# Reordering the start, the statistics, one weight load and the output products of a fused attention and gated-MLP kernel

**Chip, cores, metric.** One core of a Trainium2 chip. The metric is the device time of one execution in microseconds (us); lower is better. A profile's span is about 1.8 us shorter than the time of the same execution.

## The reference

Layernorm of x (2048 x 640, bf16), then the sum of three branches: x itself; a linear attention with 32 heads of 20; a gated MLP (640 to 1536 and back).

```python
xn = layernorm(x)                                  # over 640, no weights
q, k, v = split(xn @ wqkv)                         # 32 heads of 20
phi(t) = concat(softmax(t @ w_phi), softmax(-(t @ w_phi)))
o = (phi(q) @ (phi(k).T @ v)) / (phi(q) @ sum(phi(k)) + 1e-6)
out = x + o @ wo + (silu(xn @ w1) * (xn @ w3)) @ w2
```

## The kernel before, cut to the parts that matter

Tokens are worked in tiles of 128 (`t`, 16 of them) and chunks of 512 (`c`, four). Chunk 0 is normalized and transposed on chip by TensorE; chunks 1 to 3 are normalized, stored to DRAM and read back by a transposing DMA. A list scheduler in the kernel fixes each engine's order at build time; TensorE takes its units in program order. Six PSUM banks go around. One gate unit `GU(c, fi)` is ten products of 128x512: `gs` on VectorE frees the gate's bank.

```python
    def setup():
        ...
        for t in range(0, 4, 2):                       # x tiles 0..3, two queues
            load_x(xg[0], t // 2, 1, 0)                 # SP
            load_x(xg[0], 2 + t // 2, 1, 0, nc.scalar)  # ACT
        nc.sync.dma_start(out=wv[:], in_=wqkv3[:, :, 2 * D : 3 * D])   # V's weights, 800 KB
        load_gu(0)                                      # gate and up weights, part 0
        nc.sync.dma_start(out=wrow[:], ...)
        nc.sync.dma_start_transpose(out=wkT[:], in_=A_wqkv[:, D : 2 * D])
    def later():
        load_x(xg[1], 0, 4, 1)                          # second x chunk, 640 KB
        load_gu(2); load_gu(3)
    WARM = 11                                           # dummy products
    # ... [cut: layernorm of tile 0..3, T(t) = transposes of tile t, interleaved]
    T(0, "ACT"); T(1, "ACT")
    V(0); T(2, "DVE"); V(1); T(3, "DVE")
    plan.op("ACT", 0.5, lambda: load_gu(1, nc.scalar))  # part 1, issued from ScalarE's queue
    plan.op("SP", 0.5, later)
    V(2); V(3)
    # ... transposing load of wqT, then w2 (1.92 MB), both on SP
    fill(3 * 2.16)                                      # gate units 0..2
    for t in range(4, 8):
        ln_stats(t, ("g", 0, t // 2 - 2))               # second chunk, behind gs 0, 0, 1, 1
    for u in prep("k", wkT, wkphi, 13.0):               # folding products, ten units
        u(); fill(0.4)
    for t in range(NST):
        K(t)
        if t == 0 or t == 5 or t == 9:
            LN((t + 3) // 4 if t else 1, t)             # normalize, store, transposed read
        # ... gate units, V(t), KV(t - 2)
    KV(NST - 2)
    for g in range(4): Q(0, g)
    KV(NST - 1)
    def O(t):                                           # output tile
        for half, (lo, hi) in enumerate(zip(edges, edges[1:])):
            # 12 products with w2, then 5 with wo, into one bank, then the addition and the store
            ...
```

The softmax here doesn't subtract the row's maximum and nothing guards it: scores larger than these inputs give would overflow.

## Time and profile before

| | kernel before |
|---|---|
| median of the first 4 runs | 281.26 us (281.06 to 282.76) |
| profiled span | 279.5 us |
| TensorE busy | 270.8 us, 97% |
| TensorE idle | 8.7 us |
| first gate product | 14.69 us |

The lines themselves, and how they are read, are in the prediction. One warning for later: this is one execution, and the first 14 us of this kernel turned out to differ from execution to execution (the first gate product came at 13.79 to 17.97 us in five traces with this start).

### The profile page before, as it was taken

Reading aid. Unit: us, or ns where it says so; the run is one execution under the profiler, and the core shown is the slowest. Engines: PE = TensorE matmul, PEld = TensorE weight load, DVE = VectorE, ACT = ScalarE, POOL = GpSimd, SP = SyncE. Lnnn points to the kernel's source line nnn. Section 1 sums busy time; section 2 is a strip of 40 time slices with the busy share of each in tenths; the row PEclk is TensorE's granted clock in tenths of the full one; section 3 lists DMA queues with packets and bytes.
Section 4 is the critical chain, followed back from the end, with each engine's and each line's share of the span. In section 5 each row is a group of like instructions: output and inputs, shape, how many; then the busy total and the mean of one; then the engine's idle time right before and its main releaser. Section 6 shows DMA issues by size and latency. Waiting matters only on the chain.

```text
span 279.5 us, 4928 instructions
## 1 busy us (share of the span) xinstructions
PE 270.8 (97%) x1904; PEld 165.2 (59%) x1904; DVE 172.8 (62%) x285; ACT 147.0 (53%) x320; POOL 94.8 (34%) x124
## 2 busy tenths in 40 slices
PE   7897999999999999999999999999999999999995
PEld 2644555555566655557555577567665676467774
DVE  5507599999667974665639965732937229426421
ACT  3755776666677666667688723833228332532000
POOL 8264557775557453655212200001010110330000
PEclk9999999999999999999999999999999999999999
DMA  7999995202700060000300362261030621300311
GB/s 222 249 333 255 255 340 126 85 2 94 188 2 0 2 185 3 2 0 8 113 0 2 95 104 94 67 163 69 30 91 23 137 85 41 95 0 26 114 50 49
DMA packets 44103, 26.56 MB, mean 95 GB/s; under 512 B 26416, under 2 KB 44080, under 8 KB 44080
## 3 DMA queue, kind: packets, MB, share of 16 engines
q1 hardware_dynamic: 42336, 24.90, 33.3%
q10 hardware_dynamic: 1744, 1.34, 1.6%
q8 instruction: 15, 0.25, 0.4%
q14 instruction: 8, 0.07, 0.1%
HBM read 12.81 MB, written 7.21 MB: 72 GB/s over the span
## 4 chain that ended last, share of the span: by engine, by line
PE 80%; DVE 6%; DMA 5%; SPq 4%; ACT 2%; issue 1%; DVEq 0%; ACTq 0%
PE bank L557 31%; PE bank L801 18%; PE bank L406 12%; PE bank L805 8%; PE bank L645 6%; DMA xg<-in_A_x_dram 3%; SPq L176 3%; PE bank L691 1%; PE rtbank L691 1%; DMA oT<-od 1%; DVE gs L578 1%; DVE phik L471 1%; PE kva L490 1%; PE bank L514 1%; PE kvb L490 1%
## 5 line engine op out<-in xcount | busy, mean ns | idle before, releaser
L557 PE MATMUL bank<-xnT,w 128*128 128x512 bf16 x480 | 109.8, 379 | 0.2 <-DVE gs L578 0.2
L601 POOL TENSOR_TENSOR hT<-gs,up 128x512 bf16<-128x512 bf16 x44 | 51.2, 1164 | 139.7 <-ACT up L596 84.1
L557 PEld LDWEIGHTS <-w 128*128 128x128 bf16 x480 | 46.6, 98 | 50.4 <-issue 0.4
L801 PE MATMUL bank<-w,hT 128*128 128x320 bf16 (+2 forms) x396 | 57.9, 295 | 0.0
L573 ACT ACTIVATE th<-bank 128x512 bf16<-128x512 f32 x48 | 29.1, 607 | 36.7 <-PE bank L557 36.6
L578 DVE SCALAR_TENSOR_TENSOR gs<-th,bank 128x512 bf16<-128x512 bf16 x48 | 32.5, 676 | 24.2 <-ACT th L573 24.1
L801 PEld LDWEIGHTS <-hT 128*128 128x128 bf16 x396 | 38.0, 98 | 14.6
L406 PEld LDWEIGHTS <-xnT 128*128 128x128 bf16 x320 | 30.5, 98 | 14.0 <-issue 1.1
L810 DVE TENSOR_TENSOR res<-bank,xr 128x320 bf16<-128x320 f32 (+2 forms) x33 | 15.8, 479 | 36.3 <-PE bank L805 36.3
L596 ACT ACTIVATE up<-bank 128x512 bf16<-128x512 f32 x44 | 26.6, 603 | 22.2 <-PE bank L557 21.6
L454 DVE TENSOR_REDUCE ks<-ek 128x64 f32<-128x1280 bf16 x16 | 23.6, 1476 | 16.9 <-ACT ek L445 16.9
L471 POOL TENSOR_TENSOR phik<-ek,kr 128x640 bf16<-128x640 bf16 x16 | 29.1, 1820 | 8.4 <-PE bank L406 3.0
L699 ACT CAST rt<-bank 128x352 bf16<-128x352 f32 x32 | 13.1, 468 | 30.2 <-PE bank L691 26.4
L805 PE MATMUL bank<-wo,oT 128*128 128x320 bf16 (+2 forms) x165 | 27.1, 295 | 0.3 <-DMA oT<-od 0.3
L406 PE MATMUL bank<-wv,xnT 128*128 128x320 bf16 x160 | 24.2, 299 | 1.0 <-DMA wv<-in_A_wqkv_dram 1.0
L445 ACT ACTIVATE ek<-bank 128x320 bf16<-128x320 f32 x64 | 23.1, 437 | 3.7 <-PE bank L406 3.5
L406 PE MATMUL bank<-wkphi,xnT 128*128 128x320 bf16 x160 | 24.3, 299 | 0.0
L471 DVE TENSOR_TENSOR phik<-ek,kr 128x640 bf16<-128x640 bf16 x16 | 22.1, 1383 | 1.8 <-PE bank L406 0.5
L660 ACT ACTIVATE eq<-bank 128x512 bf16<-128x512 f32 x40 | 21.8, 601 | 2.8 <-PE bank L645 2.6
L645 PE MATMUL bank<-xnT,wqphi 128*128 128x512 bf16 x100 | 22.7, 379 | 0.0
L805 PEld LDWEIGHTS <-oT 128*128 128x128 bf16 x165 | 15.8, 98 | 6.4 <-DMA oT<-od 0.6
L287 DVE BATCH_NORM_STATS2 stats<-xg 128x6 f32<-128x320 bf16 x32 | 14.0, 471 | 6.1 <-DMA xg<-in_A_x_dram 6.1
(63 smaller groups left out, 212.6 us busy)
## 6 DMA issues: line engine op xcount, KB each, us to landing
w<-in_B_w_dram SPq DMA_DIRECT2D x6, 480.0 KB, 9.6
xr<-in_A_x_dram SPq DMA_DIRECT2D x4, 640.0 KB, 4.6
od<-om SPq DMA_DIRECT2D x8, 320.0 KB, 2.3
out_dram<-res SPq DMA_DIRECT2D x15, 160.0 KB, 1.8
w<-in_B_w_dram SPq DMA_DIRECT2D x1, 1920.0 KB, 10.8
xnd<-xn SPq DMA_DIRECT2D x3, 640.0 KB, 3.2
xg<-in_A_x_dram SPq DMA_DIRECT2D x10, 160.0 KB, 3.3
w<-in_B_w_dram ACTq DMA_DIRECT2D x2, 480.0 KB, 4.9
```

The costliest lines, as they stand in the source:

```text
L406: nc.tensor.matmul(o["ps"][:], xnT[:, c, t * P : (t + 1) * P], w[:, c, 320 * half : 320 * half + 320], start=(c == 0), stop=(c == KD - 1),)
L445: nc.scalar.activation(out=box["ek"][:, sgn, 320 * half : 320 * half + 320], in_=o["ps"][:], func=AF.Exp, scale=1.0 - 2.0 * sgn,)
L454: nc.vector.reduce_sum(out=box["s"][:].rearrange("p a h -> p (a h)"), in_=box["ek"][:].rearrange("p a (h d) -> p (a h) d", d=Dh), axis=AX.X,)
L471: phik_ins[t] = eng.tensor_mul(out=phik_b[t][:, :, sgn, :], in0=box["ek"][:, sgn, :].rearrange("p (h d) -> p h d", d=Dh), in1=box["r"][:, ...
L557: nc.tensor.matmul(o["ps"][:], w[:, k, fi * P : (fi + 1) * P], xs[:, k, :], start=(k == 0), stop=(k == KD - 1))
L573: nc.scalar.activation(out=box["th"][:], in_=og["ps"][:], func=AF.Tanh, scale=0.5)
L578: pinned["g", c, fi] = nc.vector.scalar_tensor_tensor(out=box["gs"][:], in0=box["th"][:], scalar=1.0, in1=og["ps"][:], op0=ALU.add, op1=AL ...
L596: nc.scalar.activation(out=box["up"][:], in_=ou["ps"][:], func=AF.Copy, scale=0.5)
L601: lambda: nc.gpsimd.tensor_mul(out=hT[c][:, fi, :], in0=box["gs"][:], in1=box["up"][:]),
L645: nc.tensor.matmul(o["ps"][:], wqphi[:, k, g * P : (g + 1) * P], xnT[:, k, c * 512 : (c + 1) * 512], start=(k == 0), stop=(k == KD - 1),)
L801: nc.tensor.matmul(o["ps"][:], hT[c][:, fi, ti * P : (ti + 1) * P], w2[:, fi, cols], start=(fi == 0), stop=False)
L805: nc.tensor.matmul(o["ps"][:], oT[c][:, k, ti * P : (ti + 1) * P], wo_of[0][:, k, cols], start=False, stop=(k == KD - 1))
```

## The change

Its intent is to start TensorE's useful work sooner, to take the waits out of the first 30 us, and to put ready products ahead of two later waits.

```diff
 setup():
-        for t in range(0, 4, 2):
-            load_x(xg[0], t // 2, 1, 0); load_x(xg[0], 2 + t // 2, 1, 0, nc.scalar)
-        nc.sync.dma_start(out=wv[:], ...)
+        # tile 0 in two halves, one on each queue
+        load_x(xg[0], 1, 1, 0)
+        load_x(xg[0], 2, 1, 0, nc.scalar)
+        load_wv(0)
+        load_wv(1)
+        load_x(xg[0], 3, 1, 0)
         load_gu(0)
         # wrow
+        load_gu(1)                       # now on SP, ahead of wkT
         # transposing load of wkT
         load_x(xg[1], 0, 4, 1); load_gu(2); load_gu(3)
@@ dummies: 11 -> 10, then 4 behind T(0) and 2 behind T(1); T(0) copied out in two parts
-    V(0); T(2, "DVE"); V(1); T(3, "DVE")
+    # V(0) first half, T(1), V(0) second half, V(1) first half, T(2, "ACT"), V(1) second half, T(3)
-    plan.op("ACT", 0.5, lambda: load_gu(1, nc.scalar))
@@ statistics of the second chunk
-    for t in range(4, 8): ln_stats(t, ("g", 0, t // 2 - 2))
     for u in prep("k", ...): u(); fill(0.4)
     # LN(1), the normalization of this chunk, moves from K(0) to behind the last of the gates below
+    fill((6 - gi) * 2.16)
+    for t in range(4, 8): ln_stats(t, ("g", 0, t - 2))
@@ w2
-    plan.op("SP", 0.5, <load w2>, after=36.0)
+    # behind LN(1): issued only after the transposed read of chunk 1
+            plan.op("SP", 0.5, load_w2, deps=[XT_of[4]])
@@
+    Q(0, 0)
     KV(NST - 2)
-    for g in range(4): Q(0, g)
+    for g in range(1, 4): Q(0, g)
@@ O(t), all tiles but the last
-        half 0: 12 x w2, 5 x wo;  half 1: 12 x w2, 5 x wo
+        half 0: 12 x w2;  half 1: 12 x w2;  half 0: 5 x wo;  half 1: 5 x wo
```

More of the change, by code (lines that the diff above doesn't have):

```diff
@@ L159, in load_x, with load_gu, load_wv @@
         )
-    def load_gu(i, queue=nc.sync):
+    def load_gu(i):
         for w, src in zip((w1, w3), w13):
-            queue.dma_start(out=w[:, :, 384 * i : 384 * i + 384], in_=src[:, :, 384 * i : 384 * i + 384])
+            nc.sync.dma_start(out=w[:, :, 384 * i : 384 * i + 384], in_=src[:, :, 384 * i : 384 * i + 384])
+    def load_wv(h):
+        nc.sync.dma_start(
+            out=wv[:, :, 320 * h : 320 * h + 320],
+            in_=wqkv3[:, :, 2 * D + 320 * h : 2 * D + 320 * h + 320],
+        )
     def setup():
@@ L168, in setup @@
         xg[1] = five.tile([P, 4, D], bf, name="xg", tag="five")
-        nc.vector.memset(xg[0][:, 2, 0:8], 0.0)
-        for t in range(0, 4, 2):
-            load_x(xg[0], t // 2, 1, 0)
-            load_x(xg[0], 2 + t // 2, 1, 0, nc.scalar)
-        nc.sync.dma_start(out=wv[:], in_=wqkv3[:, :, 2 * D : 3 * D])
+        nc.vector.memset(xg[0][:, 0, 320:328], 0.0)
+        nc.sync.dma_start(out=xg[0][:, 0, 0:320], in_=x2[0:P, 0:320])
+        nc.scalar.dma_start(out=xg[0][:, 0, 320:640], in_=x2[0:P, 320:640])
+        load_x(xg[0], 1, 1, 0)
[3 more added lines that the diff above has]
+        load_x(xg[0], 3, 1, 0)
         load_gu(0)
         nc.sync.dma_start(out=wrow[:], in_=A_w_phi.rearrange("h j f -> (h j) f").rearrange("(g p) f -> p g f", p=P))
+        load_gu(1)
         nc.sync.dma_start_transpose(out=wkT[:], in_=A_wqkv[:, D : 2 * D])
-    def later():
         load_x(xg[1], 0, 4, 1)
@@ L206, in warm, with dummies @@
     def warm():
-        nc.vector.memset(xnT[:, 0, 0:512], 0.0)
-        ps = bank([P, 512], f32)
-        for i in range(WARM):
-            nc.tensor.matmul(ps[:], xnT[:, 0, 0:P], xnT[:, 0, 0:512])
-    WARM = 11
+        nc.vector.memset(xnT[:, KD - 1, S - 512 : S], 0.0)
+        warm_ps.append(bank([P, 512], f32))
+        dummies(10)
+    warm_ps = []
+    def dummies(n):
+        for i in range(n):
+            nc.tensor.matmul(warm_ps[0][:], xnT[:, KD - 1, S - P : S], xnT[:, KD - 1, S - 512 : S])
     def constants():
@@ L270 @@
     rstd = consts.tile([P, NST], f32, name="rstd")
-    arrive = [3.0, 3.4, 3.8, 4.2] + [15.0] * 4
+    arrive = [3.0, 3.4, 3.8, 4.2] + [19.0] * 4
     stats_of = {}
@@ L354, in LN, with tr @@
         )
-        xt = plan.op(
-            "SP", 0.5,
-            lambda: nc.sync.dma_start_transpose(out=xnT[:, :, 512 * c : 512 * c + 512], in_=xn_d[c][:]),
-            deps=[st], lat=5.0,
-        )
+        def tr():
+            pinned["xnT", c] = nc.sync.dma_start_transpose(
+                out=xnT[:, :, 512 * c : 512 * c + 512], in_=xn_d[c][:]
+            )
+        xt = plan.op("SP", 0.5, tr, deps=[st], lat=5.0)
         for t in range(4 * c, 4 * c + 4):
@@ L375, in bank, with T, fn, ev @@
         return ringp.tile(shape, dt, name="bank", tag="bank")
-    def T(t, evac):
+    def T(t, evac, parts=((0, KD),)):
         dep = apply_of[t]
-        o = {}
-        def fn():
-            o["ps"] = bank([P, D], bf)
-            for c in range(KD):
-                nc.tensor.transpose(o["ps"][:, c * P : (c + 1) * P], xn[0][:, t, c * P : (c + 1) * P], ident[:])
-        u = plan.op("PE", pe_us(KD, P), fn, deps=[dep], takes="bank", frees=[xn_of[0]])
-        def ev():
-            dst = xnT[:, :, t * P : (t + 1) * P]
-            src = o["ps"][:].rearrange("p (c s) -> p c s", c=KD)
-            if evac == "DVE":
-                nc.vector.tensor_copy(out=dst, in_=src)
-            else:
-                nc.scalar.copy(out=dst, in_=src)
-        XT_of[t] = plan.op(evac, dve_us(D, 2) if evac == "DVE" else act_us(D), ev, deps=[u], frees=[u])
+        for lo, hi in parts:
+            o = {}
+            def fn(o=o, lo=lo, hi=hi):
+                o["ps"] = bank([P, (hi - lo) * P], bf)
+                for c in range(lo, hi):
+                    nc.tensor.transpose(
+                        o["ps"][:, (c - lo) * P : (c - lo + 1) * P], xn[0][:, t, c * P : (c + 1) * P], ident[:]
+                    )
+            u = plan.op("PE", pe_us(hi - lo, P), fn, deps=[dep], takes="bank", frees=[xn_of[0]])
+            def ev(o=o, lo=lo, hi=hi):
+                dst = xnT[:, lo:hi, t * P : (t + 1) * P]
+                src = o["ps"][:].rearrange("p (c s) -> p c s", c=hi - lo)
+                if evac == "DVE":
+                    nc.vector.tensor_copy(out=dst, in_=src)
+                else:
+                    nc.scalar.copy(out=dst, in_=src)
+            n = (hi - lo) * P
+            XT_of[t] = plan.op(evac, dve_us(n, 2) if evac == "DVE" else act_us(n), ev, deps=[u], frees=[u])
     V_of, phik_of, KV_of, phik_b, phik_a = {}, {}, {}, {}, {}
@@ L411, in proj, with V_half, V_evac, ev @@
         return plan.op("PE", pe_us(KD, 320), fn, deps=deps, takes="bank", frees=frees), o
-    def V(t, halves=(0, 1)):
-        V_of.setdefault(t, [])
-        for half in halves:
-            u, o = proj(t, wv, half, [XT_of[t]], [big_of["wv"]])
-            def ev(o=o, half=half):
-                nc.scalar.copy(
-                    out=vaug[t % 4][:, 16 * half : 16 * half + 16, 0:Dh],
-                    in_=o["ps"][:].rearrange("p (h d) -> p h d", d=Dh),
-                )
-            V_of[t].append(plan.op("ACT", act_us(320), ev, deps=[u, KV_of.get(t - 4)], frees=[u]))
+    def V_half(t, half):
+        return proj(t, wv, half, [XT_of[t]], [big_of["wv"]])
+    def V_evac(t, half, units):
+        u, o = units[t, half]
+        def ev():
+            nc.scalar.copy(
+                out=vaug[t % 4][:, 16 * half : 16 * half + 16, 0:Dh],
+                in_=o["ps"][:].rearrange("p (h d) -> p h d", d=Dh),
+            )
+        V_of.setdefault(t, []).append(
+            plan.op("ACT", act_us(320), ev, deps=[u, KV_of.get(t - 4)], frees=[u])
+        )
+    def V(t):
+        for half in range(2):
+            V_evac(t, half, {(t, half): V_half(t, half)})
     wphi_ready = {}
@@ L793, in O, with products, fn, ev @@
         edges = (0, 320, 512, 640) if last else (0, 320, 640)
-        for half, (lo, hi) in enumerate(zip(edges, edges[1:])):
-            cols = slice(lo, hi)
-            o = {}
-            def fn(o=o, cols=cols, lo=lo, hi=hi):
-                o["ps"] = bank([P, hi - lo], f32)
-                for fi in range(KF):
-                    nc.tensor.matmul(
-                        o["ps"][:], hT[c][:, fi, ti * P : (ti + 1) * P], w2[:, fi, cols], start=(fi == 0), stop=False
-                    )
-                for k in range(KD):
-                    nc.tensor.matmul(o["ps"][:], oT[c][:, k, ti * P : (ti + 1) * P], wo_of[0][:, k, cols], start=False, stop=(k == KD - 1))
-            u = plan.op("PE", pe_us(KF + KD, hi - lo), fn, deps=GU_of[c] + [dep, wo_dma], takes="bank", frees=[oT_a[c], hT_a[c]])
-            def ev(o=o, cols=cols, half=half):
-                nc.vector.tensor_tensor(out=box["res"][:, cols], in0=o["ps"][:], in1=xr[c][:, ti, cols], op=ALU.add)
+        outs = []
+        def products(half, wo):
+            lo, hi = edges[half : half + 2]
+            o = outs[half]
+            def fn():
+                if not wo:
+                    o["ps"] = bank([P, hi - lo], f32)
+                    for fi in range(KF):
+                        nc.tensor.matmul(
+                            o["ps"][:], hT[c][:, fi, ti * P : (ti + 1) * P], w2[:, fi, lo:hi],
+                            start=(fi == 0), stop=False,
+                        )
+                else:
+                    for k in range(KD):
+                        nc.tensor.matmul(
+                            o["ps"][:], oT[c][:, k, ti * P : (ti + 1) * P], wo_of[0][:, k, lo:hi],
+                            start=False, stop=(k == KD - 1),
+                        )
+            if not wo:
+                o["u"] = plan.op("PE", pe_us(KF, hi - lo), fn, deps=GU_of[c], takes="bank", frees=[hT_a[c]])
+                return
+            u = plan.op("PE", pe_us(KD, hi - lo), fn, deps=[dep, wo_dma, o["u"]], frees=[oT_a[c]])
+            def ev():
+                nc.vector.tensor_tensor(
+                    out=box["res"][:, lo:hi], in0=o["ps"][:], in1=xr[c][:, ti, lo:hi], op=ALU.add
+                )
                 if half == 1:
@@ L814, in ev @@
                 elif half == 2:
-                    nc.scalar.dma_start(out=out2[t * P : (t + 1) * P, cols], in_=box["res"][:, cols])
-            plan.op("DVE", dve_us(hi - lo), ev, deps=[u, xr_of[c], rb], frees=[u, xr_a[c]] + [rb] * (half == len(edges) - 2))
+                    nc.scalar.dma_start(out=out2[t * P : (t + 1) * P, lo:hi], in_=box["res"][:, lo:hi])
+            plan.op(
+                "DVE", dve_us(hi - lo), ev, deps=[u, xr_of[c], rb],
+                frees=[o["u"], xr_a[c]] + [rb] * (half == len(edges) - 2),
+            )
+        for half in range(len(edges) - 1):
+            outs.append({})
+            products(half, False)
+            if last:
+                products(half, True)
+        for half in range(0 if last else 2):
+            products(half, True)
     xr_of = {}
@@ L827, in residual, with load_w2 @@
         xr_of[c] = plan.op("SP", 0.5, lambda: load_x(xr[c], 0, 4, c), deps=[xr_a[c]], lat=3.5)
+    def load_w2():
+        order_after(
+            nc.sync.dma_start(out=w2[:], in_=B_w2.rearrange("(c p) d -> p c d", p=P)), pinned["xnT", 1]
+        )
     wo_of = []
@@ L841 @@
     ln_sqrt(1)
-    T(0, "ACT")
+    T(0, "ACT", ((0, 2), (2, KD)))
+    plan.op("PE", 0.8, lambda: dummies(4))
     ln_stats(2, parts=(0,))
@@ L846 @@
     ln_sqrt(2)
+    v = {(0, 0): V_half(0, 0)}
     T(1, "ACT")
+    plan.op("PE", 0.4, lambda: dummies(2))
+    v[0, 1] = V_half(0, 1)
+    V_evac(0, 0, v)
     ln_stats(3, parts=(0,))
@@ L851 @@
     ln_sqrt(3)
-    plan.op("ACT", 1.3, lambda: nc.scalar.preload_act_table(AF.Exp), deps=[rstd_of[3]])
-    V(0)
-    T(2, "DVE")
-    V(1)
+    V_evac(0, 1, v)
+    v[1, 0] = V_half(1, 0)
+    T(2, "ACT")
+    v[1, 1] = V_half(1, 1)
     ln_finish(3)
     T(3, "DVE")
-    plan.op("ACT", 0.5, lambda: load_gu(1, nc.scalar))
-    plan.op("SP", 0.5, later)
+    plan.op("ACT", 1.3, lambda: nc.scalar.preload_act_table(AF.Exp), deps=[rstd_of[3]])
+    V_evac(1, 0, v)
+    V_evac(1, 1, v)
     V(2)
@@ L864 @@
     plan.op("SP", 0.5, lambda: nc.sync.dma_start_transpose(out=wqT[:], in_=A_wqkv[:, 0:D]), after=24.0)
-    plan.op("SP", 0.5, lambda: nc.sync.dma_start(out=w2[:], in_=B_w2.rearrange("(c p) d -> p c d", p=P)), after=36.0)
     def modes(n):
@@ L885 @@
     fill(3 * 2.16)
-    for t in range(4, 8):
-        ln_stats(t, ("g", 0, t // 2 - 2))
     for u in prep("k", wkT, wkphi, 13.0):
@@ L890 @@
         fill(0.4)
+    fill((6 - gi) * 2.16)
+    for t in range(4, 8):
+        ln_stats(t, ("g", 0, t - 2))
     wq_seq = prep("q", wqT, wqphi, 34.0)
@@ L895 @@
             fetch(7 + t, t)
-        if t == 0 or t == 5 or t == 9:
-            LN((t + 3) // 4 if t else 1, t)
+        if t == 5 or t == 9:
+            LN((t + 3) // 4, t)
         fill(1.95)
+        if t == 0:
+            LN(1, ("g", 0, gi - 1))
+            plan.op("SP", 0.5, load_w2, deps=[XT_of[4]])
         if t >= 4:
@@ L908 @@
     fill(2.2)
+    Q(0, 0)
     KV(NST - 2)
-    for g in range(4):
+    for g in range(1, 4):
         Q(0, g)
```

## The prediction

> **What bounds the kernel now.** I read the engine totals first, then every wait of TensorE, then the order of work in the first 30 us, then the DMA landings there.
>
> ```profile
> PE 270.8 (97%) x1904; PEld 165.2 (59%) x1904; DVE 172.8 (62%) x285; ACT 147.0 (53%) x320; POOL 94.8 (34%) x124
> PE   7897999999999999999999999999999999999995
> DMA  7999995202700060000300362261030621300311
> ```
>
> TensorE is busy 270.8 of 279.5 us and is the only engine near full, so only two things can shorten the span: idle time of TensorE, and work that it does for nothing. The idle time is 279.5 - 270.8 = 8.7 us. The list of TensorE's waits names most of it:
>
> ```profile
> PE bank L514 <- DVE gs L578: 1.9, 1, 1.9
> PE bank L210 <- DVE xnT L207: 1.3, 1, 1.3
> PE bank L406 <- DMA wv<-in_A_wqkv_dram: 1.0, 1, 1.0
> PE bank L384 <- DVE xn L332: 0.6, 1, 0.6
> PE kva L490 <- DVE phik L471: 0.4, 1, 0.4
> PE bank L805 <- DMA oT<-od: 0.3, 1, 0.3
> PE bank L557 <- DVE gs L578: 0.2, 1, 0.2
> ```
>
> These add up to 5.7 us. The rest is the tail: TensorE's last product ends at 275.99 + 0.44 = 276.43 us, so 3.1 us of addition and store follow. 5.7 + 3.1 is the 8.7 within rounding. The work for nothing is the 11 warm-up products (4.9 us), run while the first x tile is on its way. The start, as TensorE's timeline has it:
>
> ```profile
> 1.27 4.88 PE L210 MATMUL bank<-xnT 128*128 128x512 bf16 x11 [1.27 <-DVE xnT L207]
> 5.94 0.74 PE L384 MATMUL bank<-ident,xn 128*128 128x128 bf16 x5
> 8.71 1.52 PE L406 MATMUL bank<-wv,xnT 128*128 128x320 bf16 x10 [0.98 <-DMA wv<-in_A_wqkv_dram]
> ```
>
> The first gate product starts at 14.69 us; from there TensorE is full but for the small waits. For the largest wait, the VectorE timeline shows the cause:
>
> ```profile
> 21.20 1.28 DVE L287 BATCH_NORM_STATS2 stats<-xg 128x6 f32<-128x320 bf16 x3 [3.92 <-DMA xg<-in_A_x_dram]
> 22.86 0.67 DVE L578 SCALAR_TENSOR_TENSOR gs<-th,bank 128x512 bf16<-128x512 bf16 x1
> ```
>
> VectorE stands 3.92 us at the statistics of the second x chunk, and the gate multiply behind it, which would free a PSUM bank, is held; the weight-folding products (L514) then find no bank. The DMA record of that chunk (and of V's weights):
>
> ```profile
> xg<-in_A_x_dram SPq DMA_DIRECT2D x1, 640.0 KB, 8.5
> wv<-in_A_wqkv_dram SPq DMA_DIRECT2D x1, 800.0 KB, 6.9
> ```
>
> The chunk is issued at 12.65 and lands 8.5 us later, at 21.2. V's weights are issued at 1.71 and land at 8.6.
>
> **What the Trainium skill says.** "TensorE: Matmul & The Clock Gate", Part 1, says that an N=512 product is spaced 426.7 ns while the array is cold and 215.7 ns once warm, after about 3.4 us of activity. The trace agrees: the dummies are 0.43 us apart, ten gate products take 2.16 us, and the first five transposes (0.74 us) are slower than the next five (0.45). "Perfetto Trace Analysis", Tensor Engine Instruction, says "ACT/DVE/GPSIMD are strict FIFO"; the 3.92 us stand above, with a ready gate multiply behind it, is just that. "DMA: Bandwidth & Descriptors", Queues, rings and completion order, says that SP and ACT each own one ring on each of the same 16 engines, that an engine takes turns between rings, and consumes one ring in order, though completions need not be in order. The trace fits: by 8.6 us about 2.1 MB had moved (my sum of the per-microsecond rates), while x and V's weights are only 1.47 MB, so about 0.6 MB of later loads had passed before the last byte of V's weights was in.
>
> **The change part by part.**
>
> *1. Start: loads.* x tile 0 comes in two 80 KB halves on both queues, V's weights in two halves, x tile 3 only after them. Bytes ahead of the first V half: three x tiles and 400 KB, 0.9 MB; with the same slack (a factor of 2.1/1.47) that is 1.3 MB, which had moved by about 6.2 us in the trace before. So the half should land near 6.3 instead of 8.6 (an estimate). The second half, at 1.31 MB x 1.43 = 1.87 MB, lands near 7.8. Tile 3 is then pushed to about 8.3, where before its statistics began at 7.78 without a wait.
>
> *2. Start: order on TensorE.* Now 10 dummies, tile 0's transposes, 4 dummies, V(0) first half, tile 1's transposes, 2 dummies, V(0) second half and so on. Tile 0's statistics begin perhaps 0.2 us sooner, so its transposes begin at about 5.5 and end at 6.1. Four dummies, one cold and three warm, take 0.43 + 0.65 = 1.1 us: V starts at about 7.2 instead of 8.71. But from there more stands before the first gate product: 8 V halves at 0.68 (5.4 us), three sets of transposes at 0.28 (0.84) and two dummies (0.43) are 6.7 us, against 6.0 before (8 x 0.68 + 2 x 0.28). That gives 13.9. ScalarE now also copies tile 2 (0.68 us) and still loads the Exp table (1.28 us) ahead of V(1)'s copies, in FIFO order behind tile 3's square root; six banks go around, so V(3) may wait about 0.3 us for a bank. I put the first gate product at 14.2 instead of 14.69: **gain 0.5 us** (0 to 1.3).
>
> *3. Statistics of the second x chunk.* They move from behind gates 0 and 1 to behind gates 2 to 5, and six gate units are set before the first K tile instead of five. VectorE then frees gates 0 to 2 without a hold. Only the first of these statistics still comes ahead of gate 3's multiply, which is ready at about 23. On SP, the second gate weights (two issues, 1.40 us by the first pair's duration) and the extra half loads (about 0.5) now stand ahead of the 7.28 us transpose issue, so the chunk is issued at about 14.8 instead of 12.65; but the bytes ahead of it are the same, since before the second gate weights went beside it on the ACT queue. I expect landing between 21.2 and 23.3. Landing at 21.2 costs nothing; at 23.3 the gate multiply is held until about 24.5 and the bank that the eighth folding product needs comes about 1.1 us late. So of 1.9 us about 0.5 may stay: **gain 1.4 us**.
>
> *4. K's transposed weights* are issued at about 7.5 instead of 5.32 and, with the 11.2 us of before, land at 18.7 to 19.5. They are needed after the third gate unit, 14.2 + 6 x 1.08 = 20.7. Cost 0, with about 1 us of margin.
>
> *5. Q(0,0) ahead of KV(14)* puts 1.08 us of ready products before the one that waited: **gain 0.4**. *6. Output tiles:* both halves' w2 products (2 x 1.63 us) come ahead of wo's, so the first transposed o has 1.6 us more: **gain 0.3**. The last tile keeps its order, so the tail stays 3.1 us. *7. w2's load* moves behind the first normalized transpose, at some 45 us; it is first read at 157. Cost and gain 0. The 0.2 us wait behind the later normalization I leave at 0.1 gained.
>
> Sum: 0.5 + 1.4 + 0.4 + 0.3 + 0.1 = 2.7 us. 281.26 - 2.7 = **278.6 us**, 1.0% faster.
>
> **The rivals.** (a) *The start gains all that its weights gain.* If V starts at 6.5 and no bank waits follow, the first gate product comes near 13.2, 1.5 us sooner, and the statistics' wait vanishes wholly: 281.26 - (1.5 + 1.9 + 0.8) = 277.1. For it: V's weights were the longest wait of the start. Against: TensorE's own queue from V to the gates grows by 0.7 us, and the dummies stand in it. (b) *The wait moves.* The x chunk lands late (23.5 or more), or the transposed K weights land after 20.7; TensorE then waits 1 to 2 us at the folding products as before, and only 1 us is won in all: 280.2. For it: the DMA row is at 9 of 10 in the slices up to 35 us, so putting loads in another order moves waits rather than removing them, and SP spends 7.28 us on one issue. (c) *640-byte and 80 KB pieces move slower*, tile 3 lands at 9 or later, and the square root holds ScalarE's queue: the start loses 0.5 and the whole gains about 1.7: 279.5.
>
> **Range and chances.** The sure parts (5, 6 and most of 3) are 1.5 to 2.5 us; the start adds between -0.5 and 1.5. That gives 277.2 to 280.3. Two per cent is 5.6 us. All of TensorE's waits but the tail are 5.7 us, and 1.3 of that (before the first dummy) the change does not touch; even rival (a) stays at 1.5%. So faster by over 2% has 4%, slower 2%, the rest within 2%.
>
> **What would show it.** Right: TensorE busy about 271.9 (one cold dummy fewer, -0.43, and six of which one is cold, +1.5), its wait list without L514 on gs, kva on phik and oT; V's first product at about 7.2 and the first gate product near 14.2; the x chunk landing by 23.3. Wrong: a DMA wait of TensorE at the folding products or V; a bank wait on ScalarE's V copies above 0.5 us; the first gate product after 14.7; or any new wait after 30 us, which I hold to be unchanged.

## The result, and the profile after

The changed kernel ran in 277.55 us (median of 11 runs, 277.1 to 278.91), the kernel before beside it in 281.13 (16 runs, 278.27 to 282.78). Here and below a ratio is the mean time of one kernel's fast runs over that of the other's fast runs of the same rounds, so it is not quite the ratio of the medians: 0.9903, interval 0.9871 to 0.9936. The profiled spans are 275.5 and 279.5 us. Engine totals and busy slices of the changed kernel:

```profile
PE 270.6 (98%) x1909; PEld 165.2 (60%) x1909; DVE 172.7 (63%) x284; ACT 147.2 (53%) x322; POOL 95.0 (34%) x124
PE   8999999999999999999999999999999999999995
DMA  7999829702700051001200244152220611300401
```

TensorE's dips in the second and fourth slices are gone. It is busy 270.6 us where I had written 271.9: the dummies behind the first ten and tile 0's transposes (0.44 us, 0.74 before) ran at full speed; I did not trace the rest of that difference. Its wait list has three lines left of seven:

```profile
PE bank L223 <- DVE xnT L215: 1.3, 1, 1.3
PE bank L398 <- DVE xn L343: 0.5, 1, 0.5
PE bank L581 <- DVE gs L602: 0.2, 1, 0.2
```

The start on TensorE's timeline (start, duration, both us):

```profile
5.63 1.03 PE L223 MATMUL bank<-xnT 128*128 128x512 bf16 x4
6.50 0.89 PE L423 MATMUL bank<-wv,xnT 128*128 128x320 bf16 x5
...
10.87 0.45 PE L398 MATMUL bank<-ident,xn 128*128 128x128 bf16 x5 [0.45 <-DVE xn L343]
11.16 2.88 PE L423 MATMUL bank<-wv,xnT 128*128 128x320 bf16 x20
13.88 6.64 PE L581 MATMUL bank<-xnT,w 128*128 128x512 bf16 x30
```

V starts at 6.50 and the first gate product at 13.88. VectorE's timeline and two DMA landings (last column: us from issue to landing) show the second chunk: it is issued at 15.32 and landed after 5.2 us, at 20.5, before the statistics are due, and the store of the normalized chunk lands in 3.3 us instead of 4.9:

```profile
20.10 0.69 DVE L602 SCALAR_TENSOR_TENSOR gs<-th,bank 128x512 bf16<-128x512 bf16 x1 [1.47 <-ACT th L597]
20.71 0.88 DVE L298 BATCH_NORM_STATS2 stats<-xg 128x6 f32<-128x320 bf16 x2
22.80 0.69 DVE L602 SCALAR_TENSOR_TENSOR gs<-th,bank 128x512 bf16<-128x512 bf16 x1 [0.97 <-ACT th L597]
```
```profile
xg<-in_A_x_dram SPq DMA_DIRECT2D x1, 640.0 KB, 5.2
xnd<-xn SPq DMA_DIRECT2D x1, 640.0 KB, 3.3
```

Where the 4.0 us between the two traces came from is read best from the starts of equal stages, because they need no modelled ends:

| stage start, us | before | after | gain so far |
|---|---|---|---|
| first gate product | 14.69 | 13.88 | 0.81 |
| first product of the R stage (eq times KV) | 141.89 | 138.41 | 3.48 |
| first w2 product | 157.14 | 153.67 | 3.47 |
| R products behind the first output tile | 162.67 | 158.74 | 3.93 |
| end of the last product | 276.43 | 272.50 | 3.93 |

So 0.81 us came from the start, 2.67 between gates and R (the folding wait and the wait at KV), 0.46 at the first output tile, and nothing after it. The wait list before had counted 1.94 + 0.41 and 0.28 for the last two. The difference is in how idle time is counted. In the trace before, the nine w2 products that began at 158.00 are issued 0.136 us apart, so the next could have begun at 159.22; it began at 159.67, 0.45 later, and the list shows 0.28:

```profile
158.00 1.39 PE L801 MATMUL bank<-w,hT 128*128 128x320 bf16 x9
159.67 0.85 PE L805 MATMUL bank<-wo,oT 128*128 128x320 bf16 x5 [0.28 <-DMA oT<-od]
```

So this listed wait starts at the modelled end of the product before it, some 0.17 us after the next could have been issued.

### The profile page after: what moved, and what is told of

It reads as the page before. It is cut to its first block, busy times and chain, and to the rows that moved or that the text cites. A ratio compares the mean times of both kernels' runs of the same rounds, so it can differ in the third digit from the quotient of the medians.

```text
span 275.5 us, 4940 instructions
## 1 busy us (share of the span) xinstructions
PE 270.6 (98%) x1909; PEld 165.2 (60%) x1909; DVE 172.7 (63%) x284; ACT 147.2 (53%) x322; POOL 95.0 (34%) x124
## 4 chain that ended last, share of the span: by engine, by line
PE 92%; DVE 3%; DMA 2%; SPq 1%; ACT 1%; issue 1%; DVEq 0%
PE bank L581 36%; PE bank L828 19%; PE bank L423 14%; PE bank L834 8%; PE bank L669 8%; PE rtbank L715 2%; PE bank L715 2%; DMA xg<-in_A_x_dram 2%; DVE xn L343 1%; PE bank L538 1%; PE kva L514 1%; PE kvb L514 1%; DVE phik L495 1%; DVE gs L602 0%; ACT ek L469 0%
## 5 line engine op out<-in xcount | busy, mean ns | idle before, releaser
L828 PE MATMUL bank<-w,hT 128*128 128x320 bf16 (+2 forms) x396 | 55.5, 295 | 0.0
L846 DVE TENSOR_TENSOR res<-bank,xr 128x320 bf16<-128x320 f32 (+2 forms) x33 | 15.8, 480 | 35.6 <-PE bank L834 35.6
L834 PE MATMUL bank<-wo,oT 128*128 128x320 bf16 (+2 forms) x165 | 24.7, 295 | 0.0
```

Of the source, the lines that this page charges most:

```text
L828: nc.tensor.matmul(o["ps"][:], hT[c][:, fi, ti * P : (ti + 1) * P], w2[:, fi, lo:hi], start=(fi == 0), stop=False,)
L834: nc.tensor.matmul(o["ps"][:], oT[c][:, k, ti * P : (ti + 1) * P], wo_of[0][:, k, lo:hi], start=False, stop=(k == KD - 1),)
```

## The experiments

The kernel before scatters, the changed one hardly does. In the three batches below the kernel before ran 97 times. The mean granted clock of each run splits them in two: 0.998 to 1.000, called warm here, or 0.982 to 0.994, called cold. (A mean of 0.994 over 280 us is 3.4 us at half clock. The record does not show the slow first products: in the first trace it reads 1.00 while the dummies are 0.43 us apart.) Medians in us; both kinds are mostly labelled fast, so I compare warm with warm. That split was made after the results, and it leaves out what a change does to the share of cold runs.

| kernel | warm runs: number, median, range | cold runs: number, median |
|---|---|---|
| before | 47, 280.75, 278.34 to 281.99 | 49, 282.23 |
| changed (three sets) | 21, 277.53, 277.08 to 278.91 | 0 |
| stats_only | 13, 279.62, 278.75 to 280.67 | 9, 282.14 |
| start_only | 9, 281.66, 281.24 to 282.44 | 11, 283.06 |
| late_only | 4, 279.57, 278.10 to 280.86 | 10, 281.34 |
| w2_early | 16, 278.97, 277.92 to 280.07 | 0 |
| all_but_start | 5, 277.93, 277.09 to 278.18 | 1, 283.42 |
| w2_only | 4, 280.50, 278.45 to 281.10 | 10, 282.17 |
| old_start_dummies | 9, 281.13, 279.49 to 282.06 | 5, 283.05 |
| no_fill_dummies | 3, 277.51, 277.39 to 277.72 | 0 |
| tile3_sooner | 4, 277.50, 277.36 to 277.78 | 0 |

Left out as disturbed, with no cause known: one run of the kernel before (1600.94 us), the first of no_fill_dummies (1011.57), and the first of after_third (317.56 at a clock of 0.854).

Each batch had its own chip. The warm runs of the kernel before had medians of 281.00, 279.77 and 281.00 us in the three, so a comparison across batches can be off by a microsecond.

**First batch: is the gain the sum of its parts?**

The changed kernel again:

> The changed kernel once more, on the same chip as the three partial kernels of this batch, so that their gains can be added up against its own. Both theories: ratio to the kernel before 0.986 to 0.992 (the traces differ by 4.0 us; the medians by 3.6). Stage starts as in its first trace: first gate product 13.9 us, first product of the R stage (eq times KV) 138.4, TensorE's last product ends 272.5.

277.58 us (6 runs), ratio 0.9885 (0.984 to 0.9931); first gate product 13.82. As expected.

One part at a time:

```diff
 kernel before
+ fill((6 - gi) * 2.16); ln_stats(t, ("g", 0, t - 2)) behind the folding products; LN(1) behind the last of these gates
```

> The kernel before with only the statistics of the second x chunk (and the normalization behind them, and six gate units ahead of K) placed as in the changed kernel; loads, start and output tiles as before. Theory A (each part gives what its wait cost, and they add up): the first gate product stays at 14.7, the folding products wait for no bank, and from the first gate product to the first product of the R stage 125.1 us pass instead of 127.2, so 2.1 us faster, about 279.0 beside 281.1. Rival B (the statistics' place is only safe because the new load order brings the x chunk sooner): the x chunk lands at 21.2 as before, holds the fourth gate's multiply, and a wait of 0.5 us or more stays at the folding products.

Ratio 0.9984 (0.9956 to 1.0011). The folding wait is gone, as theory A said, and rival B's remainder at the folding products did not appear; but neither theory had the wait that came instead. TensorE's wait list and timeline of this kernel:

```profile
PE bank L557 <- DMA xnT<-xnd: 1.4, 1, 1.4
```
```profile
45.20 2.32 PE L557 MATMUL bank<-xnT,w 128*128 128x512 bf16 x10
48.97 2.33 PE L557 MATMUL bank<-xnT,w 128*128 128x512 bf16 x10 [1.45 <-DMA xnT<-xnd]
```

The 13th gate unit needs the transposed second chunk, which is not there: its store took 6.7 us, because 1.92 MB of w2 were issued just ahead of it on the same queue (30.42 against 37.41 us). In this execution the x chunk itself landed at 10.88 + 4.9 = 15.8 us, not 21.2, and the first gate product came at 13.79 with the old start: the trace of the kernel before was not typical.

```diff
 kernel before
+ the changed start: loads, dummies, V's order, load_gu(1) on SP ahead of wkT
```

> The kernel before with only the start of the changed kernel (halved loads of tile 0 and of V's weights, tile 3 behind them, dummies between, V's order, second gate weights on the SP queue); statistics, output tiles and Q as before. Theory A: the first gate product at 13.9 (0.8 sooner), but the folding products wait as before, now for an x chunk that lands near 20.5, 1.8 to 2.4 us; so 0.5 to 0.9 us faster in all. Rival B (the load order alone takes the wait away, because the chunk comes sooner): the wait at the folding products falls below 1 us and the whole gains 2 us or more.

Slower than the kernel before: ratio 1.0063 (1.0036 to 1.009). Rival B is refuted. Theory A's wait at the folding products came (2.1 us), but a second wait of 0.9 us that it had not came behind it, and its small gain failed. The wait list of TensorE:

```profile
PE bank L538 <- DVE gs L602: 2.1, 1, 2.1
...
PE bank L581 <- DVE gs L602: 1.1, 2, 0.9
```

The second gate weights on SP stand ahead of the x chunk, so it lands at 15.65 + 5.2 = 20.8 us in this trace; with the statistics in their old place that stalls VectorE, and TensorE waits twice. With the same load order the changed kernel's chunk landed at 20.5 us and nothing waited, so the statistics' new place is what makes the new load order bearable. The clock fell behind the two waits; from the stages of this trace (columns: stretch, length, then busy time and instructions of PE, PEld, DVE, ACT, POOL, then granted clock, DMA share, GB/s):

```profile
23.00:25.00 2.00, 1.40 (x8) 0.64 (x8) 2.00 (x8) 0.74 (x2) 1.15 (x1) 1.00 1.11 328
25.00:27.00 2.00, 1.44 (x4) 0.55 (x4) 1.18 (x3) 0.28 (x1) 1.20 (x2) 0.52 1.29 208
27.00:29.00 2.00, 2.00 (x21) 1.50 (x20) 0.00 (x0) 1.05 (x3) 1.58 (x3) 0.63 1.32 292
```

```diff
 kernel before
+ Q(0, 0) ahead of KV(14); w2 products of both halves ahead of wo's
```

> The kernel before with only the late parts: one Q unit ahead of KV(14), and both halves' w2 products ahead of wo's in all output tiles but the last. Theory A: no wait of TensorE on phik at KV and none on the transposed o; the steps between stage starts shorten by about 0.57 (KV) and 0.46 (first output tile), 1.0 us in all, more than the 0.41 and 0.28 that the wait list counts, because it counts idle time only from the modelled end of the product before. Rival B: it gains only the 0.7 us of the wait list.

Ratio 0.9996 (0.9966 to 1.0026): unclear on time. In its trace the waits at KV and at the first output tile are gone, as theory A said. But only 4 of its 14 runs were warm, and the scatter of the first 50 us, larger than 1 us, hides the gain. The stage starts settle the output tile: from the first product of the R stage to the R products behind the first output tile 20.32 us pass, against 20.78 in the first trace of the kernel before, so 0.46 less, as theory A said. The trace again has a wait for the transposed chunk, 0.6 us, which the first trace of the kernel before had not.

So the parts alone give, warm against warm of the same batch (before 281.00), 1.4, -0.7 and 1.4 us, 2.1 in sum, and the whole 3.4. Something was missing, and the chunk's wait pointed to w2. (late_only's share of this rests on four warm runs of 278.10 to 280.86 us.)

**Second batch: w2, the start, and the scatter.**

```diff
 changed kernel
- load_w2 behind the transposed read of chunk 1
+ load_w2 where the kernel before has it
```

> The changed kernel with one DMA moved back: w2 (1.92 MB) is issued on the SP queue where the kernel before has it, ahead of the store of the second normalized chunk. All other instructions stand in the order of the changed kernel. Theory C (formed from the first batch: w2 stands in the way of that chunk's store and transpose, which the statistics-only kernel waited for 1.4 us): the store lands after 6 to 7 us instead of 3.3, the transposed chunk near 49 instead of 45.7 us, and TensorE waits for it about 1.4 us at the 13th gate unit; so 278.8 to 279.3, with runs scattered over 2 us or more. Rival, the step of the prediction (w2's place costs and gains nothing): as the changed kernel, 277.6.

278.96 us, ratio 0.9935 (0.9905 to 0.9965). The changed kernel was not in this batch; against its 277.53 in the others, on other chips, that is 1.4 us slower, with every other instruction in the same order. In the same batch it is 1.0 us slower than the warm runs of all_but_start (277.93, below), which has the late w2 and even the old start. The wait that w2 makes, from its wait list and its landings:

```profile
PE bank L581 <- DMA xnT<-xnd: 0.8, 1, 0.8
```
```profile
xnd<-xn SPq DMA_DIRECT2D x1, 640.0 KB, 6.0
```

Theory C holds, with 0.8 us listed in the one execution profiled where I expected 1.4. By stage starts it is 1.0: 125.54 us from the first gate product to the first R product, against 124.53 in the changed kernel's first trace. In the finished kernel the step "cost and gain 0" of the prediction is thus refuted.

```diff
 changed kernel
- the changed start
+ the start of the kernel before (load_gu(1) again on the ACT queue)
```

> The changed kernel with the start of the kernel before (whole loads, 11 dummies, second gate weights on the ACT queue late); statistics, w2, Q and output tiles as changed. Theory A (the start is worth the 0.8 us between the first two traces): about 278.4. Theory C (the start of the kernel before is as fast when its DMA goes well, 13.8 us to the first gate product in two of three traces, and the statistics' place is what makes the loads' order harmless): 277.4 to 278.0, with a wider scatter than the changed kernel.

277.99 us (6 runs); the five warm ones have a median of 277.93, 0.4 us above the changed kernel's of the other batches, hardly more than the scatter between them; the sixth was cold, 283.42. The first gate product at 14.43 in this trace, against 13.82 to 14.21 in five traces of the changed start (tile3_sooner's among them), says the same. The five warm runs favour theory C. But the changed kernel did not run on this chip, where the kernel before was 1.2 us faster too, so 0.4 is not secured as the start's worth in warm runs. Whether a cold run is what the start guards against is taken up below.

```diff
 kernel before
- load w2 at its old place
+ load w2 behind the transposed read of chunk 1
```

> The kernel before with w2's load behind the transpose of the second normalized chunk, nothing else moved. Theory C: the chunk's store lands in about 3.3 us, no wait for it is left in any run, but the wait at the folding products (up to 2 us, in runs where the x chunk lands late) is; 0.3 to 1.0 us faster on the median. Rival (w2's place alone carries the gain): 2 us or more faster.

281.79 us, ratio 1.0021 (0.9981 to 1.0061), no gain: 10 of 14 runs were cold, and its profile fell in the slow state (285.01 us). Theory C's 0.3 to 1.0 us was not seen; the rival's 2 us is excluded. In that one execution the store landed in 4.0 us and nothing waited for the chunk, as theory C said, nor did the folding products wait; TensorE's two longest waits were for other loads:

```profile
PE bank L559 <- DMA w<-in_B_w_dram: 1.8, 1, 1.8
PE bank L408 <- DMA wv<-in_A_wqkv_dram: 1.8, 1, 1.8
```

With w2_early this says that w2's place is worth about 1 us in the finished kernel and nothing measurable alone; that earlier waits cover it there was not tested by itself.

> The kernel before, profiled once more on this chip. Its times scatter from 278.3 to 286.2 us, the changed kernel's from 277.2 to 278.1. Theory C: what differs from its first trace is when loads land: V's weights near 7 us instead of 8.6, so the first gate product at 13.8; the second x chunk at 16 to 18 us instead of 21.2, so no wait at the folding products; and then a wait of 0.5 to 2 us for the transposed second chunk, which its first trace does not have. Theory A: the waits of its first trace, again.

282.61 us, granted clock 0.992. Theory C was right that the waits would differ and that the folding wait would be gone, and wrong about the rest: V's weights came still later, and nothing waited for the transposed chunk. The wait list, TensorE's timeline and two stretches of this execution:

```profile
PE bank L406 <- DMA wv<-in_A_wqkv_dram: 2.4, 1, 2.4
```
```profile
7.20 0.45 PE L384 MATMUL bank<-ident,xn 128*128 128x128 bf16 x5 [0.51 <-DVE xn L332]
10.00 2.55 PE L406 MATMUL bank<-wv,xnT 128*128 128x320 bf16 x10 [2.35 <-DMA wv<-in_A_wqkv_dram]
...
17.97 6.64 PE L557 MATMUL bank<-xnT,w 128*128 128x512 bf16 x30
```
```profile
8.00:10.00 2.00, 0.00 (x0) 0.00 (x0) 1.37 (x5) 1.20 (x4) 0.00 (x0) 1.00 0.97 279
10.00:12.00 2.00, 2.00 (x9) 1.19 (x9) 0.00 (x0) 1.50 (x2) 0.00 (x0) 0.58 1.50 106
```

The same load of V's weights took 5.2, 5.3, 6.7, 6.9, 7.2 and 8.3 us in six traces with this start (the slow one left out). At 8.3 us TensorE stood idle 2.9 us with 0.45 us of work between, the clock fell to half, ten V products took 2.55 us instead of 1.52, and the first gate product came at 17.97, 3.3 us later than in the first trace. The whole lost only 1.3 us against it, for the second chunk, due at 18.7 us here, was then no longer waited for. In this execution a late load early on hid a late load later. That this is why single parts measured so little fits these traces; no run tests it by itself.

**Third batch: are the dummies needed, and is there a better start?**

```diff
 changed kernel
- dummies(4) behind T(0), dummies(2) behind T(1)
```

> The changed kernel without the six dummies behind the first two sets of transposes; nothing else differs on any engine. Theory D (formed from the first two batches: half of the runs of the kernel before, and none of the changed one, have a mean granted clock of 0.994 or less, because TensorE stands idle near 3 us around the first V product and the clock then falls to half): the weights now come early enough that the gaps stay below 1.5 us in all, so the clock is 0.998 or more in all runs and the time is the changed kernel's, 277.3 to 277.8. Rival E (the dummies keep the clock up): runs at 0.994 appear, 1.5 to 2.5 us longer. Rival F (each dummy costs its 0.215 us on the path): up to 1.3 us faster.

277.39, 277.51 and 277.72 us, all at clock 1.0, beside 277.08 to 277.53 of the changed kernel on the same chip. Theory D holds as far as three runs go: the dummies neither cost nor are shown to be needed. In the changed kernel's traces they stand where TensorE would wait anyway, for tile 0's copy and V's second half. This kernel's only profile fell in the disturbed execution of 1009.8 us, so no trace shows it.

```diff
 all_but_start
+ dummies(6) between T(1) and V(0)
```

> The kernel with everything changed but the start (loads of the kernel before), and six dummies (1.3 us) between tile 1's transposes and the first V product, where TensorE waits for V's weights. Theory D: the idle time around V falls below 2 us also when the weights come at 10 us, so no run falls under 0.998; runs with early weights pay up to 1.3 us: 278.0 to 280.0 in all runs. Rival (late weights alone make the slow runs, the clock is only a sign of them): runs of 282 us and more remain, with a clock of 0.994 or less or without.

281.66 us, and 5 of 14 runs still cold: theory D failed here, and the rival's runs of 282 us and more remain (six of 14). In the profiled execution V began at 9.12 at full speed, but a new wait came. TensorE's wait list, and ScalarE's queue with the two issues of the second gate weights:

```profile
PE bank L562 <- DMA w<-in_B_w_dram: 2.3, 1, 2.3
```
```profile
12.32 0.39 ACTq L163 DMA_DIRECT2D w<-in_B_w_dram  x1
16.14 0.39 ACTq L163 DMA_DIRECT2D w<-in_B_w_dram  x1
16.56 1.42 ACT L424 CAST vaug<-bank 128x320 bf16<-128x320 f32 x4 [3.73 <-PE bank L562]
```

With the old start, part 1 of the gate weights is issued from ScalarE's queue among the copies of V's products. In the first trace of the kernel before the two issues came at 11.90 and 12.33. Here the second came at 16.14, and the fourth gate unit then waited 2.3 us for that load. V's lateness does not account for it: V began only 0.41 us later than there, the first issue 0.42. ScalarE stood still for 3.73 us until just behind the second issue, and V's remaining copies came only then; what held the issue no trace shows.

Where V is later, the issues follow its copies: in before_again (V at 10.00) both came at 14.87 or later, and in w2_only's profiled run (a slow one, V at 9.67) at 15.42 or later, with the wait of 1.8 us shown there. The changed kernel issues this load on SP near 6 us, where no compute stands ahead of it. So the old start has a second weak place, a load issued among compute. This kernel does not isolate the clock, and what the clock alone costs stays an estimate, (1 - 0.994) x 281 = 1.7 us for one cold stretch. Nor does it show what the six dummies cost: all_but_start without them ran on another chip.

```diff
 changed kernel
-        load_wv(1); load_x(xg[0], 3, 1, 0)
+        load_x(xg[0], 3, 1, 0); load_wv(1)
```

> The changed kernel with x tile 3 loaded ahead of V's second half instead of behind it (one pair of DMA issues changes places on SP, no other engine's order changes). TensorE waits 0.45 to 0.5 us for tile 3's normalization in two of four traces of this start. If that sets the first gate product: tile 3 lands near 7.5 instead of 8.1 to 8.5 us, V's second half near 8.2 instead of 7.7, the first gate product moves from 13.8-14.2 to about 13.6, and the kernel gains 0.1 to 0.4 us over the changed one. Rival: the second V half then waits for its weights by as much, and nothing is gained.

277.50 us, nothing gained over 277.46 beside it: the rival was right. Its trace has no wait for tile 3 left, but the second V half waits a little for its weights (0.13 us by the starts; the wait list shows none), issue at 2.75 and landing 5.9 us later, and the first gate product is at 13.99.

> The changed kernel beside the three above, on the same chip and in the same rounds: 277.2 to 278.9, all runs at a clock of 0.998 or more.

277.46 us; besides the disturbed first run, 277.08 to 277.53. No version beat the changed kernel.

## Why the prediction was right

It said 278.6 (277.2 to 280.3) and within 2%; measured 277.55, 1.0% faster by ratio. The mechanism was mostly right, its sizes were too small, and one step was wrong. How near the forecast gain of 2.7 us came depends on the measure: 2.7 between the means of fast runs, 3.6 between the medians, 4.0 between the two traces. With a kernel before that scatters by several microseconds, the close agreement of the first is partly luck.

- **Start (0.5).** Landings were well estimated: V's first half 6.1 us for 6.3, the second 7.7 for 7.8, tile 3 8.1 for 8.3. V began at 6.50, not 7.2: tile 0's transposes began at 5.36 for 5.5 and were issued in 0.27 us for 0.6, and the four dummies all ran warm, 0.87 us for 1.1. And the bank wait for V(3) did not come, a wait of 0.45 for tile 3 did. The first gate product at 13.88 for 14.2 makes the gain 0.81 between the two traces. But the reference point, 14.69, was one draw: other traces with the old start's instructions have 13.79, 13.82, 14.43 and 17.97. In warm runs all_but_start puts the start's worth at about 0.4, across chips and so not secured. That the start also keeps the clock up shows in the counts: with the statistics in their new place, none of 44 runs with the changed start was cold (the changed kernel, w2_early, no_fill_dummies, tile3_sooner), and 15 of 42 with the old start were (stats_only, all_but_start, old_start_dummies). With the statistics in their old place the changed start had 11 cold runs of 20. Which part of the start does it was not taken apart, but the six dummies were not needed in three runs. The prediction had no such effect.
- **Statistics (1.4).** The wait was predicted to shrink to 0.5; it vanished. The chunk was issued at 15.32 (predicted 14.8) but landed at 20.5, sooner than the 21.2 to 23.3 that I took. The step mis-sized is that remainder of 0.5, and the 1.9 itself is 2.1 counted by stage starts.
- **K's transposed weights (0).** Right in the landing, 9.46 + 9.4 = 18.9, needed at 20.35, but by two errors that cancelled: the issue was expected at 7.5, and the second pair of gate weights ahead of it took 3.18 us to issue, not 1.40; the landing then took 9.4 us, not 11.2. The chunk's issue at 15.32 is luck of the same kind: the transposing issue ahead of it took 5.81 us, not 7.28.
- **Q ahead of KV (0.4) and the output tiles (0.3).** Right in kind; by stage starts KV's share is 2.67 less 2.1, about 0.57, and the output tile's 0.46. The wait list I took them from counts from modelled ends.
- **w2 ("Cost and gain 0").** Wrong. The step looked only at when w2 is read, 157 us, not at what stands behind it on its queue. The store of the second chunk did; w2_early lost 1.0 to 1.4 us by it. The first trace before has no wait for that chunk, so it could not show this.
- **The later wait (0.1).** It stayed: 0.2 us before and after.
- **Rivals.** (a) was nearer than the forecast: it said 277.1, V began at the 6.5 us that it supposed, and the statistics' wait vanished wholly as it said; only its first gate product, 13.2, was too early (13.88). (c) did not come: tile 3 landed at 8.1, not 9. (b), that the wait moves to another load, did not happen to the whole, but it happened to each part alone: in stats_only to the transposed chunk, in start_only back to the folding products. The prediction added the parts; alone they gave 2.1 of 3.4 us.
- **The warm-up, read from the Trainium skill.** The spacings agree with the trace, the 3.4 us only roughly: in the trace before all eleven dummies were still 0.43 us apart, the last begun 4.3 us after the first.

## What to carry to other kernels

When loads saturate the start of a kernel, profile the unchanged kernel several times before trusting any wait of it, and look at the spread of its times and its granted clock: a wait that one trace lacks may be there in half of the runs. Judge a DMA's place by what is queued behind it, not only by when its data is read, and expect that taking one wait away shows the next; test such parts by taking one out of the finished change as well as by adding one to the old kernel. Ready work ahead of a product that waits for DMA gains a little more than the wait list says.

## What the Trainium skill lacked or had wrong

- "TensorE: Matmul & The Clock Gate", HAM oscillation, gives the rule of no TensorE gaps longer than about 3.4 us. The next section of that page lets short frequent idles do the same, but gives no length. Shorter ones sufficed here: gaps of 0.51 and 2.35 us with 0.45 us of work between them (before_again, clock 0.58 in the next 2 us), and of 2.09 and 0.92 us with 1.4 between (start_only, clock 0.52). A single gap of 1.94 us did not (first trace before), nor one of 2.3 (old_start_dummies).
- "DMA: Bandwidth & Descriptors", Issuing engines are not separate DMA queues, says that issuing on several engines only saves the sequencer's time to issue. It lacks the cost that these runs show: an issue on ScalarE's queue stands among ScalarE's own work, at 11.90 us where V began at 8.71 and at 14.87 where V began at 10.00 (before, before_again); at 15.42 TensorE waited 1.8 us for the load (w2_only, a slow run). Nor does the page say how wide landings scatter when the queue is full: the same 800 KB load, in the same place, took from 5.2 to 8.3 us over six traces.
- "Perfetto Trace Analysis", Tensor Engine Instruction, says that a product's end is an estimate. It does not say what follows for waits: idle time counted from that end was 0.28 us where the stage starts show 0.45.
